# Two spectral and attention layers on one core: row blocks turned by transposing transfers instead of TensorE, and one of GpSimd's pieces moved within its batch

## The chip, the core and the metric

The kernel runs on one NeuronCore of a Trainium2 chip. Its engines work side by side and meet at semaphores: TensorE (PE; PEld is its weight load), VectorE (DVE), ScalarE (ACT), GpSimd (POOL) and SyncE (SP), whose queue issues transfers. The metric is the device time of one execution in microseconds (us). Lower is better.

## The reference

One sequence of 2048 rows with 512 columns in bf16 goes through two equal pairs of layers, each layer added to its input after a layer norm:

```python
x = x + _A_ref(_layernorm(x), A_w_r, A_w_i)               # 2-D real FFT, filter, inverse FFT
x = x + _B_ref(_layernorm(x), B_wq, B_wk, B_wv, B_wo)     # attention
# _B_ref: 32 query heads of 16 columns, one key head and one value head shared by all
scores = einsum("bhqd,bkd->bhqk", q, k) * 16 ** -0.5
p = softmax(scores); o = einsum("bhqk,bkd->bhqd", p, v); out = o @ wo
```

The two lines run twice with the same weights.

## The kernel before

Everything stays on chip between load and store. `x_sb` holds the rows as 4 (r) x 4 (t) tiles of 128x512. A "row block" is the four tiles of one t, 512 rows. The program has four stages: spectral layer, attention, spectral layer, attention. "Pair 0" is the first two, "pair 1" the last two.

**The end of a spectral layer** is `blocks` (L973 to L1059). For each row block t, TensorE does the last inverse transform (`odd`, `even`, L318 and L336), ScalarE copies one half out of PSUM (L325), VectorE joins the halves and adds the residual (`rows_out`, L353, L355). For the attention behind it, each block then needs its layer norm: statistics by VectorE (`stats`, L105 and L106, once per tile), the root by ScalarE (L109), scale and shift by VectorE (`scales`, L113, L114), and the normalised rows themselves, tile by tile, by ScalarE (L129) or VectorE (L131) as `put` is told. The rows must be turned, columns to partitions, before they can be multiplied by the weights. `transposed` (L384) does half a block: eight 128x128 transposes on TensorE into one PSUM bank (L389) and a copy of 1024 columns to `xT` by the engine it is given (L392). `keys` (L394) makes the keys of a block with four matmuls (L401), which ScalarE writes to `KT` (L403); the function that it returns has VectorE take the largest key (`kmax`, L404). `values` (L406) makes the values with 16 small matmuls (L412) and four scaled copies on ScalarE (L414). `first_queries` (L416) makes the queries of the first head group, which VectorE copies out (L421). ScalarE loads the table for the exponential at L1051. `ready` (L423) makes the factor kq from the four maxima and scales the first queries with it (L425 to L427). No score can be made before that. 

The order of TensorE, ScalarE and VectorE in a spectral layer is the order of the program's lines; an engine waits in place for what its next instruction needs. Transfers that SP issues also go out in program order. PSUM has eight banks, in `blocks` three double banks (`p2`) and two single banks (`mm`). `xT` and `Z`, the input of the transform over rows, are two views of the same 16 KB per partition, `xz`.

**The attention** (`run`, L429) has 32 head groups per pair: four query blocks of 512 queries by eight groups of four heads. A head group has 64 tiles of 128 keys x 512 queries. For 45 of them ScalarE takes the exponential from PSUM (L635), in 18 steps of three and two tiles in turn; a step is the unit of the written schedule. The other 19 are done without it: VectorE turns a score into a bit pattern (`t_new`, L669), and the tile counts as the weighted sum of four images of this pattern, shifted against each other. The pattern itself is the first. Images 1 and 2 are made by VectorE for a whole batch of tiles at once (`s_new`, L684, at the batch's steps 0 and 3). The last image is made by GpSimd, tile by tile (`pool_new`, L688); these are its *pieces*. Each piece has a dependence on the latest image by VectorE (`pace`, L550), so a piece never starts before that image has ended. The 19 tiles come in three batches of 6, 7 and 6 tiles, six steps each (`DPOS`, `BSTEPS`; the first group lacks the first batch). TensorE multiplies every tile and every image with the values (`pv_step`, L648), each a fixed number of steps after it was listed: the images of a tile are listed by `share` (L485, L492), and the result is due two steps later (`LAG`).

Pieces are dealt to the six steps by the same `share`, which rounds down: batches of seven get 1, 1, 1, 1, 1, 2. Beside pieces GpSimd normalises the output of the group before (`od_new`, L580); in odd groups VectorE then turns the outputs of two groups back (`ot_new`, L586), between images 1 and 2 of the seven-tile batch. TensorE makes the queries of the next group (L370) and, in groups 9 to 12, 17 to 20 and 25 to 28, the output projection of a finished query block (L599), whose sums VectorE adds to `x_sb` (L604).

Of the kernel before, what the change touches and what calls it, by code (L numbers as in the profile page):

```python
# [12 lines left out]
P = 128  # L13
# [13 lines left out]
BSTEPS = 6  # L27
# [330 lines left out]
class Attention:  # L358
    def __init__(self, nc, tc, tabs, norm, x_sb, xz, KT, aw, small):
        self.nc, self.tc, self.tabs, self.norm, self.x_sb, self.KT, self.aw, self.small = nc, tc, tabs, norm, x_sb, KT, aw, small  # L360
        self.xT = xz.rearrange("p (c a) (b n) -> p c (a b) n", c=NC, b=4)
        self.Z = xz.rearrange("p (i t) d -> p t i d", t=T)
        self.kmax = small.tile([P, NQB], F32, tag="kmax", bufs=1)
        self.kq = small.tile([P, 2], F32, tag="kb", bufs=1)
        self.QT = {}

    def qproj(self, g, ps, cs=range(NC)):
        qb, hg = divmod(g, HG)
        for c in cs:
            self.nc.tensor.matmul(ps, lhsT=self.aw["wq"][:, c, hg, :], rhs=self.xT[:, c, 4 * qb:4 * qb + 4, :].rearrange("d k p -> d (k p)"),  # L370
                                  start=(c == 0), stop=(c == NC - 1))

    def qcast(self, ps):
# [10 lines left out]
    def transposed(self, psum, t, xn, half, engine):  # L384

        ps = psum.tile([P, 2, NC, P], BF, tag="mm", bufs=2)
        for i in range(2):
            for c in range(NC):
                self.nc.tensor.transpose(ps[:, i, c, :], xn[:, 2 * half + i, c * P:(c + 1) * P], self.tabs["EYE"][:, 0, :])  # L389
        k = 4 * t + 2 * half  # L390
        copy = engine.copy if engine is self.nc.scalar else engine.tensor_copy
        copy(out=self.xT[:, :, k:k + 2, :].rearrange("d c i p -> d i c p"), in_=ps)  # L392

    def keys(self, psum, t):  # L394

        nc, aw = self.nc, self.aw
        k0, k1 = 4 * t, 4 * t + 4
        two = psum.tile([P, 2, 512], F32, tag="p2", bufs=3)
        ps = two[:, 0, 0:(k1 - k0) * P]
        for c in range(NC):  # L400
            nc.tensor.matmul(ps, lhsT=aw["wk"][:, c, :], rhs=self.xT[:, c, k0:k1, :].rearrange("d k p -> d (k p)"),  # L401
                             start=(c == 0), stop=(c == NC - 1))
        nc.scalar.activation(out=self.KT[:, k0 * P:k1 * P], in_=ps, func=ACT.Identity, bias=self.tabs["KAB"][:, 1:2], scale=self.tabs["KAB"][:, 0:1])  # L403
        return lambda: nc.vector.tensor_reduce(out=self.kmax[:, t:t + 1], in_=ps, axis=mybir.AxisListType.X, op=ALU.max, apply_absolute_value=True)  # L404

    def values(self, psum, t):  # L406
        nc, aw = self.nc, self.aw
        two = psum.tile([P, 2, 512], F32, tag="p2", bufs=3)
        psv = two[:, 0, 0:4 * DH].rearrange("p (i d) -> p i d", d=DH)
        for i in range(4):  # L410
            for c in range(NC):
                nc.tensor.matmul(psv[:, i, :], lhsT=self.xT[:, c, 4 * t + i, :], rhs=aw["wv"][:, c, :], start=(c == 0), stop=(c == NC - 1))  # L412
# [16 lines left out]
    def run(self, row_done, work, psums):  # L429
# [242 lines left out]
        def image_step(n):  # L672
            if n in d_phase:
                g, b, k, tiles = d_phase[n]
                src, nt = tb[(g, b)].bitcast(I16), len(tiles)
                if k == 0:
                    pool_new = work.tile([P, NBT, 512], I16, tag="SP", bufs=2)
                    sb[(g, b, 3)] = pool_new
                if k in IMG:
                    i = 1 + IMG.index(k)  # L680
                    s_new = work.tile([P, NBT, 512], I16, tag="S", bufs=3)
                    sb[(g, b, i)] = s_new
                    lo = POOL2 if i == 2 else 0
                    image[0] = nc.vector.tensor_scalar(out=s_new[:, lo:nt, :], in0=src[:, lo:nt, :], scalar1=PH_OFF[i], scalar2=None, op0=ALU.add)  # L684
                    if lo:
                        pace(nc.gpsimd.tensor_scalar(out=s_new[:, 0:lo, :], in0=src[:, 0:lo, :], scalar1=1.0, scalar2=PH_OFF[i], op0=ALU.mult, op1=ALU.add))
                for i in share(nt, k):
                    pace(nc.gpsimd.tensor_scalar(out=sb[(g, b, 3)][:, i, :], in0=src[:, i, :],  # L688
                                                 scalar1=1.0, scalar2=PH_OFF[3], op0=ALU.mult, op1=ALU.add))

# [58 lines left out]
def full_kernel(ctx, tc, A_x, A_w_r, A_w_i, B_x, B_wq, B_wk, B_wv, B_wo, out, n_pairs=2):  # L749
# [37 lines left out]
    Z = xz.rearrange("p (i t) d -> p t i d", t=T)  # L787

    def weights(tmp):
        wq_raw = tmp.tile([P, 4, D], BF, tag="x4", bufs=3)  # L790
# [182 lines left out]
    def blocks(work, sp, psum, att):  # L973
# [6 lines left out]
        def new_rows():  # L980
            X_new = work.tile([P, 4, 512], BF, tag="x4", bufs=3)
            return X_new
# [6 lines left out]
            for r in rows:  # L989
                norm.stats(x_sb[:, r, t, :], r, t)  # L990

        def rows_scaled(t):
            norm.scales(t)
            X = new_rows()
            put(t, X, (A, D, A, A))
            return X

        def turn(t, xn):
            att.transposed(psum, t, xn, 0, A)
            att.transposed(psum, t, xn, 1, A)  # L1000

        sp.odd(0)
        sums(0)
# [5 lines left out]
        sp.rows_out(1)  # L1009
        sp.odd(2)  # L1010
        sums(2)
        xn0 = rows_scaled(0)
        stats(1)
        norm.root(1)
        sp.rows_out(2)
        sp.odd(3)
        sums(3)
        xn1 = rows_scaled(1)
        stats(2)
        att.transposed(psum, 0, xn0, 0, A)  # L1020
        norm.root(2)
        att.transposed(psum, 0, xn0, 1, A)
        bound0 = att.keys(psum, 0)
        sp.rows_out(3, (0,))
        stats(3, (0, 1))
        att.transposed(psum, 1, xn1, 0, A)
        norm.root(3, slice(0, 2))
        att.transposed(psum, 1, xn1, 1, A)
        sp.rows_out(3, (1,))
        norm.scales(2)  # L1030
        xn2 = new_rows()
        put(2, xn2, (D,) * 4)
# [18 lines left out]
        nc.scalar.activation(out=dmyo, in_=norm.eps, func=ACT.Exp)  # L1051
# [118 lines left out]
```

## Time and profile before

| | |
|---|---|
| runs of this kernel | 1563.38, 1563.37, 1562.22 us; median 1563.37 |
| the profiled execution | 1565.87 us |
| its span, first to last instruction | 1564.1 us |
| first attention, first to last exponential | 119.98 to 787.4 us |
| second attention | 884.50 to 1552.4 us |
| row blocks, last normalised block to first exponential | 93 to 120 us and 858 to 884.5 us |
| granted TensorE clock, mean | 0.983 |

The profile is of one execution, taken by the hardware. A timeline line gives the start from the span's beginning, the length, the engine, the line of the kernel, the operation, what it writes and reads, how many such instructions were merged, and in brackets how long the engine had been idle and what ended that. The chain of waits is followed back from the last instruction, at each step to what released it.

### The profile page before, as it was taken

How to read it: one execution, taken by the hardware profiler on the slowest of the kernel's cores; microseconds unless marked ns; L12 is line 12 of the kernel's file. 1: busy time of each engine (PE TensorE's matmuls, PEld its weight loads, DVE VectorE, ACT ScalarE, POOL GpSimd, SP SyncE). 2: the span in 40 equal slices, each digit the busy share in tenths (PEclk: the TensorE clock that was granted, in tenths of full speed). 3: DMA queues.
4: the chain of work that ended last, by engine and by line, in shares of the span. 5: the costliest groups of instructions: out<-in, count | busy, mean ns of one | idle time of the engine just before them, and what ended most of it. 6: DMA issues, size and time to landing. Idle time of an engine off the chain costs nothing.

```text
span 1564.1 us, 33013 instructions
## 1 busy us (share of the span) xinstructions
PE 1349.6 (86%) x13145; PEld 429.5 (27%) x13252; DVE 1420.6 (91%) x2279; ACT 1442.9 (92%) x1361; POOL 797.0 (51%) x1310
## 2 busy tenths in 40 slices
PE   5888888899888988898889788888998899889987
PEld 2442222222222222222234322222222222222222
DVE  6687999999999999999987889999999999999995
ACT  6659999999999999999965799999999999999996
POOL 1003555565656655665600055556556656666564
PEclk9997999999999999999999899999999999999998
DMA  8000000000000000000010000000000000000000
GB/s 278 16 1 1 2 2 1 1 1 2 1 2 1 1 1 2 1 2 1 1 41 1 1 1 2 2 1 5 5 2 5 5 4 5 5 5 5 5 5 18
DMA packets 13198, 17.21 MB, mean 11 GB/s; under 512 B 5748, under 2 KB 10484, under 8 KB 12788
## 3 DMA queue, kind: packets, MB, share of 16 engines
q1 hardware_dynamic: 12660, 14.05, 2.7%
q8 instruction: 103, 1.69, 0.4%
q0 software_dynamic: 384, 1.05, 0.2%
q14 instruction: 51, 0.42, 0.1%
HBM read 13.00 MB, written 2.10 MB: 10 GB/s over the span
## 4 chain that ended last, share of the span: by engine, by line
DVE 35%; ACT 31%; issue 14%; PE 12%; POOL 4%; DVEq 0%; POOLq 0%; ACTq 0%
ACT e L635 30%; DVE t_new L669 16%; DVE s_new L684 9%; POOL pool_new L688 4%; PE pv_new L648 4%; PE sc L546 3%; DVE st L105 1%; PE new L203 1%; DVE o L565 1%; DVE qt L376 1%; DVE ot_new L586 1%; PE dv L546 1%; PE new L294 1%; PE new L242 1%; DVE dst L353 1%
## 5 line engine op out<-in xcount | busy, mean ns | idle before, releaser
L635 ACT ACTIVATE e<-sc 128x1536 bf16<-128x1536 f32 (+1 forms) x1158 | 1316.6, 1293 | 21.7 <-PE dv L546 17.4
L688 POOL TENSOR_SCALAR pool_new<-t_new 128x512 int16<-128x512 int16 x1204 | 748.5, 644 | 719.9 <-DVE s_new L684 630.4
L669 DVE TENSOR_SCALAR t_new<-dv 128x512 uint16<-128x512 f32 x1204 | 791.5, 677 | 76.3 <-PE dv L546 61.7
L648 PE MATMUL pv_new<-e,vaug 128*32 128x512 bf16 x2892 | 595.6, 389 | 0.0
L546 PE MATMUL sc<-qt,KT 32*128 32x512 bf16 x2892 | 459.2, 388 | 115.0 <-ACT e L635 108.5
L546 PE MATMUL dv<-qt,KT 32*128 32x512 bf16 x1204 | 455.3, 387 | 21.8 <-DVE t_new L669 20.2
L648 PE MATMUL pv_new<-s_new,vaug 128*32 128x512 bf16 x2408 | 422.5, 386 | 5.9 <-DVE s_new L684 5.9
L684 DVE TENSOR_SCALAR s_new<-t_new 128x3584 int16<-128x3584 int16 (+1 forms) x380 | 386.3, 1017 | 0.1
L648 PE MATMUL pv_new<-pool_new,vaug 128*32 128x512 bf16 x1204 | 299.8, 387 | 20.8 <-POOL pool_new L688 20.8
L546 PEld LDWEIGHTS <-KT 32*128 32x128 bf16 x4096 | 156.7, 91 | 561.0 <-issue 559.4
L648 PEld LDWEIGHTS <-vaug 128*32 128x32 bf16 x7708 | 154.3, 94 | 399.3 <-issue 368.3
L648 PE MATMUL pv_new<-t_new,vaug 128*32 128x512 bf16 x1204 | 232.7, 387 | 0.0
L370 PE MATMUL ps<-xz,wq_sb 128*128 128x512 bf16 x186 | 61.5, 386 | 4.1 <-DVE t_new L669 0.4
L565 DVE STREAM_TRANSPOSE o<-pv_new 128x512 f32<-128x512 f32 x64 | 45.2, 706 | 12.2 <-PE pv_new L648 12.2
L203 PE MATMUL new<-tab_F,xz 128*128 128x512 bf16 x186 | 48.2, 404 | 3.5 <-DVE xz L167 3.3
L376 DVE TENSOR_SCALAR qt<-ps,kq 128x512 bf16<-128x512 f32 x62 | 46.0, 742 | 1.2 <-PE ps L370 1.2
L105 DVE BATCH_NORM_STATS2 st<-x_sb 128x6 f32<-128x512 bf16 x64 | 42.9, 671 | 3.6 <-DMA x_sb<-in_A_x_dram 3.5
L580 POOL TENSOR_TENSOR od_new<-o,den 128x256 bf16<-128x256 f32 x62 | 38.5, 620 | 0.0
L267 DVE TENSOR_TENSOR m<-x_new,wt 128x1024 bf16<-128x1024 bf16 x32 | 20.7, 687 | 14.3 <-ACT x_new L243 14.3
L243 ACT CAST x_new<-new 128x1024 bf16<-128x1024 f32 x16 | 16.2, 1012 | 18.4 <-PE new L242 17.0
L370 PEld LDWEIGHTS <-wq_sb 128*128 128x128 bf16 x256 | 22.0, 97 | 31.5 <-issue 16.7
L336 PE MATMUL new<-G_new,t_new 128*128 128x512 bf16 x128 | 29.9, 379 | 0.5 <-DVE G_new L303 0.4
(106 smaller groups left out, 582.0 us busy)
## 6 DMA issues: line engine op xcount, KB each, us to landing
tab_F<-const_F SPq DMA_DIRECT2D x5, 640.0 KB, 11.7
x_sb<-in_A_x_dram SPq DMA_DIRECT2D x4, 512.0 KB, 4.8
t_new<-const_IE SPq DMA_DIRECT2D x2, 1024.0 KB, 7.3
rt<-in_A_w_r_dram SPq DMA_DIRECT2D x1, 1028.0 KB, 8.4
rt<-in_A_w_i_dram SPq DMA_DIRECT2D x1, 1028.0 KB, 12.7
t_new<-const_IO SPq DMA_DIRECT2D x2, 512.0 KB, 3.3
out_dram<-x_sb SPq DMA_DIRECT2D x8, 128.0 KB, 2.0
out_dram<-x_sb POOLq DMA_DIRECT2D x8, 128.0 KB, 2.3
```

The lines of the kernel that those rows point to most:

```text
L105: self.nc.vector.bn_stats(st, x_ap)
L203: self.mm(ps, lhsT=z, rhs=tab, start=start and i == 0, stop=stop and i == len(mms) - 1)
L370: self.nc.tensor.matmul(ps, lhsT=self.aw["wq"][:, c, hg, :], rhs=self.xT[:, c, 4 * qb:4 * qb + 4, :].rearrange("d k p -> d (k p)"), start= ...
L376: self.nc.vector.tensor_scalar(out=qt, in0=ps, scalar1=self.kq[:, 1:2], scalar2=None, op0=ALU.mult)
L546: nc.tensor.matmul(dst, lhsT=KT[hs, kc * P:(kc + 1) * P], rhs=QT[g][hs, :], start=True, stop=True)
L565: nc.vector.transpose(out=o.rearrange("p c j -> p (c j)"), in_=ps)
L580: return engine.tensor_tensor(out=turned_od[g // 2][:, :, half], in0=o[:, :, 0:DH], in1=den.unsqueeze(2).broadcast_to([P, 16, DH]), op=ALU ...
L635: nc.scalar.activation(out=e[:, 0:na, :], in_=sc[:, 0:na, :], func=ACT.Exp, scale=SCALE)
L648: nc.tensor.matmul(pv[g][32 * h:32 * h + 32, :], lhsT=vaug[:, max(j, 0), kc, :], rhs=rhs, start=(first_pv[(g, h)] == u), stop=(last_pv[(g, ...
L669: nc.vector.tensor_scalar(out=tb[(g, b)][:, i, :], in0=dv, scalar1=T_MUL, scalar2=T_ADD, op0=ALU.mult, op1=ALU.add)
L684: image[0] = nc.vector.tensor_scalar(out=s_new[:, lo:nt, :], in0=src[:, lo:nt, :], scalar1=PH_OFF[i], scalar2=None, op0=ALU.add)
L688: pace(nc.gpsimd.tensor_scalar(out=sb[(g, b, 3)][:, i, :], in0=src[:, i, :], scalar1=1.0, scalar2=PH_OFF[3], op0=ALU.mult, op1=ALU.add))
```

## The change

Three things change, and the layout that they need.

1. Row blocks 0, 1 and 2 are turned by two transfers each (`turned_rows`), which SP issues and which transpose on the way from the normalised rows to `xT`; block 3 stays with `transposed`. In blocks 0 and 1 all four tiles are now normalised by ScalarE, in block 2 by VectorE, ScalarE, VectorE, ScalarE. The first half of block 3 is copied by ScalarE instead of VectorE. Keys, maxima, values and first queries are put in another order around it.
2. The pieces of a batch are dealt rounding up: batches of seven get 2, 1, 1, 1, 1, 1; batches of six are as before. When TensorE uses them does not change.
3. `values` takes a single bank (`mm`) instead of a double one (`p2`).

`xT` is now laid out by block of 128 rows first, so a half block is one contiguous run of 1024 columns, and the rows that `keys` and `qproj` read are four runs of 128 instead of one of 512. `Z` is laid out so that a row block of it still shares its place with the same row block of `xT`.

```diff
-        self.xT = xz.rearrange("p (c a) (b n) -> p c (a b) n", c=NC, b=4)
-        self.Z = xz.rearrange("p (i t) d -> p t i d", t=T)
+        self.xT = xz.rearrange("p k (c n) -> p k c n", c=NC)
+        self.Z = xz.rearrange("p (t i) d -> p t i d", t=T)
...
+    def turned_rows(self, t, xn, half):
+
+        rows, k = slice(2 * half, 2 * half + 2), 4 * t + 2 * half
+        self.nc.sync.dma_start(out=self.xT[:, k:k + 2, :, :].rearrange("d i c p -> d (i c) p"), in_=xn[:, rows, :].rearrange("p i d -> p (i d)"), transpose=True)
...
     def values(self, psum, t):
-        two = psum.tile([P, 2, 512], F32, tag="p2", bufs=3)
-        psv = two[:, 0, 0:4 * DH].rearrange("p (i d) -> p i d", d=DH)
+        psv = psum.tile([P, 4, DH], F32, tag="mm", bufs=2)
...
-                for i in share(nt, k):
+                for i in range(-(-nt * k // BSTEPS), -(-nt * (k + 1) // BSTEPS)):
                     pace(nc.gpsimd.tensor_scalar(out=sb[(g, b, 3)][:, i, :], in0=src[:, i, :],
...
+        def rows_turned(t, engines):
             norm.scales(t)
             X = new_rows()
+            for half in range(2):
+                put(t, X, engines[2 * half:2 * half + 2], (2 * half, 2 * half + 1))
+                att.turned_rows(t, X, half)
...
-        xn0 = rows_scaled(0)
+        rows_turned(0, (A,) * 4)
         stats(1)
         norm.root(1)
         sp.rows_out(2)
         sp.odd(3)
         sums(3)
-        xn1 = rows_scaled(1)
+        rows_turned(1, (A,) * 4)
+        bound0 = att.keys(psum, 0)
         stats(2)
-        att.transposed(psum, 0, xn0, 0, A)
         norm.root(2)
-        att.transposed(psum, 0, xn0, 1, A)
-        bound0 = att.keys(psum, 0)
         sp.rows_out(3, (0,))
         stats(3, (0, 1))
-        att.transposed(psum, 1, xn1, 0, A)
         norm.root(3, slice(0, 2))
-        att.transposed(psum, 1, xn1, 1, A)
         sp.rows_out(3, (1,))
-        norm.scales(2)
-        xn2 = new_rows()
-        put(2, xn2, (D,) * 4)
+        rows_turned(2, (D, A, D, A))
+        att.values(psum, 0)
         norm.scales(3, slice(0, 2))
         xn = new_rows()
         put(3, xn, (D, D), (0, 1))
-        att.values(psum, 0)
         bound1 = att.keys(psum, 1)
         stats(3, (2, 3))
-        att.transposed(psum, 2, xn2, 0, A)
         norm.root(3, slice(2, 4))
-        att.transposed(psum, 2, xn2, 1, A)
+        att.transposed(psum, 3, xn, 0, A)
+        query = att.first_queries(psum)
         bound0()
-        att.transposed(psum, 3, xn, 0, D)
+        att.values(psum, 1)
         norm.scales(3, slice(2, 4))
         put(3, xn, (D, D), (2, 3))
+        att.transposed(psum, 3, xn, 1, D)
         bound1()
-        query = att.first_queries(psum)
         bound2 = att.keys(psum, 2)
-        att.transposed(psum, 3, xn, 1, D)
+        query()
         dmyo = small.tile([P, 1], F32, tag="dmyo", bufs=1)
         nc.scalar.activation(out=dmyo, in_=norm.eps, func=ACT.Exp)
-        query()
-        att.values(psum, 1)
         bound = att.keys(psum, 3)
+        att.qabs(att.QT[0])
         bound2()
-        att.qabs(att.QT[0])
         bound()
```

More of the change, by code (lines that the diff above doesn't have):

```diff
@@ L369, in qproj @@
         for c in cs:
-            self.nc.tensor.matmul(ps, lhsT=self.aw["wq"][:, c, hg, :], rhs=self.xT[:, c, 4 * qb:4 * qb + 4, :].rearrange("d k p -> d (k p)"),
+            self.nc.tensor.matmul(ps, lhsT=self.aw["wq"][:, c, hg, :], rhs=self.xT[:, 4 * qb:4 * qb + 4, c, :],
                                   start=(c == 0), stop=(c == NC - 1))
@@ L391, in transposed @@
         copy = engine.copy if engine is self.nc.scalar else engine.tensor_copy
-        copy(out=self.xT[:, :, k:k + 2, :].rearrange("d c i p -> d i c p"), in_=ps)
+        copy(out=self.xT[:, k:k + 2, :, :], in_=ps)
+    def turned_rows(self, t, xn, half):
+        rows, k = slice(2 * half, 2 * half + 2), 4 * t + 2 * half
+        self.nc.sync.dma_start(out=self.xT[:, k:k + 2, :, :].rearrange("d i c p -> d (i c) p"), in_=xn[:, rows, :].rearrange("p i d -> p (i d)"), transpose=True)
     def keys(self, psum, t):
@@ L400, in keys @@
         for c in range(NC):
-            nc.tensor.matmul(ps, lhsT=aw["wk"][:, c, :], rhs=self.xT[:, c, k0:k1, :].rearrange("d k p -> d (k p)"),
+            nc.tensor.matmul(ps, lhsT=aw["wk"][:, c, :], rhs=self.xT[:, k0:k1, c, :],
                              start=(c == 0), stop=(c == NC - 1))
@@ L407, in values @@
         nc, aw = self.nc, self.aw
-        two = psum.tile([P, 2, 512], F32, tag="p2", bufs=3)
-        psv = two[:, 0, 0:4 * DH].rearrange("p (i d) -> p i d", d=DH)
+        psv = psum.tile([P, 4, DH], F32, tag="mm", bufs=2)
         for i in range(4):
             for c in range(NC):
-                nc.tensor.matmul(psv[:, i, :], lhsT=self.xT[:, c, 4 * t + i, :], rhs=aw["wv"][:, c, :], start=(c == 0), stop=(c == NC - 1))
+                nc.tensor.matmul(psv[:, i, :], lhsT=self.xT[:, 4 * t + i, c, :], rhs=aw["wv"][:, c, :], start=(c == 0), stop=(c == NC - 1))
         for j in range(4):
@@ L786, in full_kernel @@
     out_v = out.flatten_outer_dims().rearrange("(r p t) d -> p r t d", r=R, p=P, t=T)
-    Z = xz.rearrange("p (i t) d -> p t i d", t=T)
+    Z = xz.rearrange("p (t i) d -> p t i d", t=T)
     def weights(tmp):
@@ L990, in stats @@
                 norm.stats(x_sb[:, r, t, :], r, t)
-        def rows_scaled(t):
+        def rows_turned(t, engines):
             norm.scales(t)
             X = new_rows()
[L995 to L1000, printed above, removed]
+            for half in range(2):
+                put(t, X, engines[2 * half:2 * half + 2], (2 * half, 2 * half + 1))
+                att.turned_rows(t, X, half)
         sp.odd(0)
```

## The prediction

> **What bounds the kernel now.** I read the page's sections 1, 2 and 4 first, then the waits of ScalarE and TensorE, then the chain of waits and the timelines in two places: one pair of head groups in the attention, and the end of the row blocks before it.
>
> ```profile
> PE 1349.6 (86%) x13145; PEld 429.5 (27%) x13252; DVE 1420.6 (91%) x2279; ACT 1442.9 (92%) x1361; POOL 797.0 (51%) x1310
> ...
> ACT e L635 30%; DVE t_new L669 16%; DVE s_new L684 9%; POOL pool_new L688 4%; PE pv_new L648 4%; PE sc L546 3%; DVE st L105 1%; PE new L203 1%; DVE o L565 1%; DVE qt L376 1%; DVE ot_new L586 1%; PE dv L546 1%; PE new L294 1%; PE new L242 1%; DVE dst L353 1%
> ```
>
> ScalarE is the fullest engine, and its exponentials (L635) lead the chain that ended last; but GpSimd, busy for 51% only, stands in that chain with 4%, some 60 us. An engine that is half idle is there because others wait for it. From the waits (who waited for whom: us in total, times, longest):
>
> ```profile
> PE pv_new L648 <- POOL pool_new L688: 20.8, 24, 1.3
> ...
> ACT e L635 <- PE dv L546: 17.4, 24, 1.5
> ```
>
> In the trace's single records 18 of TensorE's 24 waits are 0.98 us long, nine in each attention (181, 222, 264, 306 us and so on), all in odd head groups; 0.8 us after each, ScalarE stands idle for 0.63. One of them, first as the chain of waits (start, length, what), then the last two of those pieces in GpSimd's timeline, then ScalarE's timeline:
>
> ```profile
> 300.87 0.98 DVE s_new L684
> 301.86 0.07 issue
> 301.93 3.08 POOL pool_new L688 x4
> 305.00 0.04 issue
> 305.05 0.40 PE pv_new L648 x4
> ```
> ```profile
> 303.09 0.62 POOL L688 TENSOR_SCALAR pool_new<-t_new 128x512 int16<-128x512 int16 x1
> 303.68 1.32 POOL L688 TENSOR_SCALAR pool_new<-t_new 128x512 int16<-128x512 int16 x1
> ```
> ```profile
> 302.87 2.38 ACT L635 ACTIVATE e<-sc 128x1536 bf16<-128x1536 f32 x2
> 305.88 1.45 ACT L635 ACTIVATE e<-sc 128x1536 bf16<-128x1536 f32 x1 [0.63 <-PE dv L546]
> ```
>
> Four pieces follow VectorE's second image (L684, at 300.80) of the seven-tile batch. Three run at 0.59 us each; the fourth starts while VectorE makes the next image (303.56, 0.96 long) and takes 1.32. TensorE wanted it at 305.05 - 0.98 = 304.07. So ScalarE's steps at 302.87, 304.20, 305.88 are 1.33 and 1.68 us; in the single records a 1024-wide exponential is else followed after 0.90. A stall costs 1.677 - 0.903 = 0.774 us.
>
> The row blocks are another matter. From 97 to 115 us the chain of waits is VectorE almost alone (L105, L353, L131); then, in the timelines of ScalarE and VectorE:
>
> ```profile
> 113.94 0.78 ACT L403 ACTIVATE KT<-two,tab_KAB 128x512 bf16<-128x512 f32 x1 [1.11 <-PE two L401]
> 114.73 1.28 ACT L1051 ACT_TABLE_LOAD   x1
> ...
> 116.79 0.78 ACT L403 ACTIVATE KT<-two,tab_KAB 128x512 bf16<-128x512 f32 x1
> ```
> ```profile
> 117.60 0.69 DVE L404 TENSOR_REDUCE kmax<-two 128x1 f32<-128x512 f32 x1 [1.07 <-ACT KT L403]
> ...
> 118.83 0.35 DVE L427 TENSOR_SCALAR qt<-qt,kq 128x512 bf16<-128x512 bf16 x1
> ```
>
> Keys of block 3, their maximum, the factor kq, the first queries: the attention starts at 119.98. The second pair repeats this to 0.1 us, ending at 884.50.
>
> **Pieces 2, 1, 1, 1, 1, 1.** Same instructions, same TensorE order; one piece moves from behind image 2 to ahead of it. Behind image 2 stand three pieces: the last ends at 303.09 + 0.62 = 303.71, before 304.07 and without meeting the next image. All 18 stalls have this pattern to 0.01 us. VectorE can carry the faster pace: it is busy for 38.4 of the 41.5 us between two stalls. Sum: 18 x 0.774 = **-13.9 us**; nothing, if another wait takes the place; -9.7, if each leaves a step of the 0.23 us kind that ends the groups with an output projection (349.28). I take the full sum.
>
> The cost is ahead of image 2. In odd groups five GpSimd operations (four pieces, one normalisation) would end 4.25 us after image 1, image 2 starts at 4.34: free. In even groups image 2 starts 3.72 after image 1 and meets the fifth (3.6 to 4.2). The nearest row is at 776.62: an image that met a running piece took 1.48 instead of 1.08. So 30 images come some 0.45 late. Cover: VectorE idles 0.21 to 0.56 two instructions later (282.64), and the next image loses its own meeting with the fourth piece (1.24 down to 0.95, at 324.38); TensorE needs that image 0.2 earlier, but then waits 0.20 for ScalarE anyway (281.75). I take 0; without the cover 30 x 0.25 = +7.5.
>
> **Row blocks, by transfer.** Per pair TensorE loses 48 of 64 transposes (L389; 6.6 of 8.8 us in all). ScalarE loses five of six copies (L392, 1.00 each) and gains four normalisations (L129, 0.71 apart). VectorE, the bound, loses four normalisations (L131, 0.33 apart) and one of two copies (0.60): 1.9 us. SyncE gains six transfers of 256 KB; an issue takes it 0.3 to 0.6 us, its queue is otherwise done since 45 us, and the tables of the next pair behind them go out at 786. Walk, with L for issue to landing:
> - Block 0: ScalarE normalises 93.45 to 96.4; the halves land by 96.4 + L. TensorE is busy with sums until 101.2, so keys 0 wait only if L > 4.8. Behind them on TensorE stands everything else.
> - Block 1: ends 102.2, lands 102.2 + L; keys 1 end near 107.3 for L = 4, and ScalarE's KT follows.
> - Block 2: VectorE reaches its scales at 106.4 (before 107.09); ScalarE ends its two rows at 108.35; landing 108.35 + L.
> - Block 3: VectorE's last rows end at 111.9 (before 113.81), TensorE transposes until 112.5, so keys 2 start at the later of 112.5 and 108.35 + L. Keys 2 (1.05), KT (0.78), table load (1.28), dmyo, KT of block 3 (0.78), maximum and factor (1.5) follow in one row: the queries are ready at 118.2 instead of 119.18, 1.0 us earlier, up to L = 4.15; each us of L beyond costs one.
>
> No row shows a transposing transfer. Nearest rows: 128 KB out takes 1.7 to 3.0 us, 512 KB in (IO, x) 3.3 and 4.8; far end, the eight small wka transfers of short runs, issued in a row over 11.22 us, 1.40 each. With 16 blocks of 128x128 in a row block that would be 22 us. I take L = 4.5, by the 512 KB rows: 0.6 per pair, **-1.2 us**; from -2 (L under 4.15) to +34 (22 us: 22 - 4.15 - 1.0 = 17 later per pair).
>
> The Trainium skill has rules on both sides. "Advanced Engine Details and Errata", section "X-Bar Transpose (TRN2)", says that transposing transfers are as fast as plain ones; by it the sum stands. "VectorE: DVE Perf Modes", section "The three transpose paths", gives 1309 ns for one 128x128 block; 16 in a row would be an estimate of 21 us, and the time some 1582. No run here shows either yet.
>
> **Values in single banks, layout.** Values 0 is scaled away (0.55) by 108.9, before values 1 wants its bank near 111: 0; uncovered 0.55 per pair. The rows read by L370 become four runs of 128 instead of one: no row of the trace has such an operand; 0, at worst four matmuls per group slowed as at half clock (0.39 to 0.61), 0.9 us under the 1.7 us per group that TensorE waits for ScalarE (108.5 / 62).
>
> **Clock.** TensorE has 0.50 of its clock from 117.8 for 13.65 us and from 1544.6 for 10.2. Less transposing may bring the first forward: keys at 0.61 instead of 0.38, some +1 per pair. The last may shift either way, some 3 us. Both inside the range.
>
> **Sum.** -13.9 - 1.2 = -15.1. The profiled execution took 1565.87 (span 1564.1, 1.8 around it), 2.5 above the median of 1563.37: 1550.8 beside it, **1548.3** beside the median.
>
> **Rivals.**
> - *The transfers land late* (slower). If blocks of 128x128 are served one after another, keys 2 hold TensorE until 108.35 + L. It decides from L = 12: then each pair loses 6.9 and eats the gain. At 22 us: 1563.4 - 13.9 + 34 = 1583. For it: the wka rows; against: the plain rows. Chance 0.10. Half-way cases (L 6 to 10, 1551 to 1559): 0.07.
> - *VectorE pays in odd groups too.* The fifth operation (3.64 to 4.25) runs beside L586, the transposition of od_new (0.70), which never met GpSimd before. If that waits as an image does, image 2 is 0.5 late, and TensorE, which already waits 0.19 for it, stalls there; some 0.3 of the 0.77 is left: 1563.4 - 5.4 - 1.2 = 1556.8. Against it: L565, the other transposition, runs beside pieces without stretching them. 0.10.
> - *The change does not free the stall*, because TensorE waits for an earlier piece: 1562. 0.05; the end of the wait, 0.06 after the fourth piece, speaks against it.
>
> Forecast 0.68. About 0.2% (3.1 us) can be told from no change. Faster 0.83 (forecast, half-way cases, odd groups less a little), same 0.07, slower 0.10. Range 1545 to 1560: it takes in the clock's 3 us, the uncovered images and the half-way cases; it leaves out the late transfers and the unfreed stall.
>
> **What would show it.** TensorE's waits for pool_new fall from 24 to about 6, and ScalarE's steps of 1.68 vanish; images 2 of even groups take about 1.5; six transfers per pair land in 4 to 5 us; first exponential near 119.4. I am wrong if keys 2 wait for a transfer by more than 2 us, if another stall of 0.6 us stands in the odd groups, or if the late images of the even groups reach ScalarE.

## The result, and the profile after

The changed kernel takes **1545.61 us** (median of four runs, 1545.29 to 1547.75), beside 1562.80 (1560.60 to 1563.38, four runs) for the kernel before on the same chip: ratio 0.9895, 95% interval 0.9878 to 0.9913. 17.2 us were gained; 15.1 were forecast, as 1548.3. The result lies inside the stated range, close to its lower end.

In the kernel after, most lines behind the diff's first part stand four further down: L635 is L639, L684 is L688, L688 is L692. The matmuls and the copy of `keys` (L401, L403) are L406 and L408, the table load (L1051) is L1046. First the same lines as before, from the page of the kernel after: the engines' busy time, and the lines of the chain that ended last.

```profile
PE 1348.7 (87%) x13115; PEld 427.4 (28%) x13156; DVE 1421.1 (92%) x2269; ACT 1435.7 (93%) x1359; POOL 778.3 (50%) x1310
...
ACT e L639 36%; DVE t_new L673 15%; DVE s_new L688 8%; PE sc L550 2%; PE pv_new L652 2%; DVE st L105 1%; PE new L203 1%; DVE o L569 1%; DVE qt L376 1%; DVE ot_new L590 1%; PE new L294 1%; PE dv L550 1%; PE new L242 1%; DVE dst L353 1%; DVE x_sb L353 1%
```

GpSimd's pieces, 4% of the chain before, are no longer among its lines. The waits of the kernel after (who for whom: us in total, times, longest) say the same:

```profile
PE two L406 <- DMA xz<-X_new: 7.7, 4, 2.7
...
ACT e L639 <- PE dv L550: 4.5, 4, 1.5
...
PE pv_new L652 <- POOL pool_new L692: 1.4, 3, 0.6
```

TensorE's 24 waits for pieces (20.8 us) are 3 (1.4 us), and ScalarE's 24 (17.4) are 4. The first line shown is new: TensorE waits four times for a transposing transfer, 2.7 us ahead of keys 1 and 0.9 to 1.3 ahead of keys 2.

One odd head group of the kernel after, GpSimd's and VectorE's timelines (start, length, engine, line, operation, how many merged):

```profile
294.20 1.20 POOL L692 TENSOR_SCALAR pool_new<-t_new 128x512 int16<-128x512 int16 x2 [1.37 <-PE ps L370]
295.37 0.62 POOL L584 TENSOR_TENSOR od_new<-o,den 128x256 bf16<-128x256 f32 x1
295.95 1.24 POOL L692 TENSOR_SCALAR pool_new<-t_new 128x512 int16<-128x512 int16 x2
```
```profile
296.66 0.70 DVE L590 STREAM_TRANSPOSE ot_new<-od_new 128x512 bf16<-128x512 bf16 x1
297.28 1.05 DVE L688 TENSOR_SCALAR s_new<-t_new 128x3584 int16<-128x3584 int16 x1
```

The fifth operation ahead of image 2 ends at 295.95 + 1.24 = 297.19, 0.09 before the image (0.08 to 0.09 in all 30 odd groups that have one). It ran beside L590, and neither was stretched: 0.62 and 0.70 us as ever.

Now the end of the row blocks, as TensorE and ScalarE saw it in the kernel after:

```profile
104.09 1.02 PE L406 MATMUL two<-xz,wka 128*128 128x512 bf16 x4 [2.72 <-DMA xz<-X_new]
...
112.41 3.30 PE L406 MATMUL two<-xz,wka 128*128 128x512 bf16 x8 [1.30 <-DMA xz<-X_new]
```
```profile
114.33 0.78 ACT L408 ACTIVATE KT<-two,tab_KAB 128x512 bf16<-128x512 f32 x1 [3.72 <-PE two L406]
115.12 1.28 ACT L1046 ACT_TABLE_LOAD   x1
...
116.53 0.76 ACT L408 ACTIVATE KT<-two,tab_KAB 128x512 bf16<-128x512 f32 x1
```

Keys 2 (112.41) wait 1.30 us for block 2's last transfer, and then take long: keys 2 and 3 are merged in that line. By stages, in the two profiled executions:

| stage, us | before | after | difference |
|---|---|---|---|
| start to the first normalised row block | 93.40 | 92.20 | -1.2 |
| row blocks, pair 0: from there to the first exponential | 26.58 | 27.50 | +0.9 |
| first attention, to its last exponential | 667.39 | 659.16 | -8.2 |
| from there to the second pair's first normalised block | 70.56 | 70.62 | +0.1 |
| row blocks, pair 1 | 26.57 | 26.80 | +0.2 |
| second attention | 667.88 | 657.38 | -10.5 |
| after the last exponential | 11.72 | 9.92 | -1.8 |

The first stage's difference is no effect of the change: in the second profile of the same kernel (see below) the first normalised block starts at 93.57. TensorE's longest wait for an input load is 9.6 us in the profile after and 10.7 in the one before. The sum of the differences is -20.5, more than the 17.2 of the medians, because the profiled execution of before (1565.87) was 3.1 us above the median of 1562.80. So: **the attention gained, and the row blocks gained nothing in these two profiles.**

### The profile page after: what moved, and what is told of

Same layout as the page of the kernel before. It is cut to its first block, busy times and chain, and to the rows that moved or that the text cites. A ratio compares the mean times of both kernels' runs of the same rounds, so it can differ in the third digit from the quotient of the medians.

```text
span 1543.6 us, 32910 instructions
## 1 busy us (share of the span) xinstructions
PE 1348.7 (87%) x13115; PEld 427.4 (28%) x13156; DVE 1421.1 (92%) x2269; ACT 1435.7 (93%) x1359; POOL 778.3 (50%) x1310
## 2 busy tenths in 40 slices
DMA packets 25870, 20.35 MB, mean 13 GB/s; under 512 B 18420, under 2 KB 23156, under 8 KB 25460
## 3 DMA queue, kind: packets, MB, share of 16 engines
q0 software_dynamic: 384, 1.05, 0.2%
## 4 chain that ended last, share of the span: by engine, by line
ACT 38%; DVE 33%; issue 16%; PE 10%; DMA 1%; POOL 0%; DVEq 0%; POOLq 0%; ACTq 0%
ACT e L639 36%; DVE t_new L673 15%; DVE s_new L688 8%; PE sc L550 2%; PE pv_new L652 2%; DVE st L105 1%; PE new L203 1%; DVE o L569 1%; DVE qt L376 1%; DVE ot_new L590 1%; PE new L294 1%; PE dv L550 1%; PE new L242 1%; DVE dst L353 1%; DVE x_sb L353 1%
## 5 line engine op out<-in xcount | busy, mean ns | idle before, releaser
L639 ACT ACTIVATE e<-sc 128x1536 bf16<-128x1536 f32 (+1 forms) x1158 | 1312.8, 1306 | 6.4 <-PE dv L550 4.5
L692 POOL TENSOR_SCALAR pool_new<-t_new 128x512 int16<-128x512 int16 x1204 | 727.7, 626 | 723.0 <-DVE s_new L688 635.6
L652 PE MATMUL pv_new<-e,vaug 128*32 128x512 bf16 x2892 | 583.9, 386 | 0.0
L688 DVE TENSOR_SCALAR s_new<-t_new 128x3584 int16<-128x3584 int16 (+1 forms) x380 | 393.1, 1035 | 0.1
L370 PE MATMUL ps<-xz,wq_sb 128*128 128x512 bf16 x248 | 65.1, 385 | 0.6 <-DVE t_new L673 0.4
L243 ACT CAST x_new<-new 128x1024 bf16<-128x1024 f32 x16 | 16.2, 1012 | 18.4 <-PE new L242 17.0
```

The costliest lines, as they stand in the source:

```text
L639: nc.scalar.activation(out=e[:, 0:na, :], in_=sc[:, 0:na, :], func=ACT.Exp, scale=SCALE)
L652: nc.tensor.matmul(pv[g][32 * h:32 * h + 32, :], lhsT=vaug[:, max(j, 0), kc, :], rhs=rhs, start=(first_pv[(g, h)] == u), stop=(last_pv[(g, ...
```

## The experiments

"Pieces alone" means the new dealing without the transfers, and so on. All ratios are to the kernel before, timed beside it on the same chip; the runs stand in four series, and the kernel after itself took 1545.61 in one and 1547.01 in another, so medians of different series are compared to 1 or 2 us only.

**The two halves apart.** The kernel before with the new dealing alone:

```diff
-                for i in share(nt, k):
+                for i in range(-(-nt * k // BSTEPS), -(-nt * (k + 1) // BSTEPS)):
```

> The kernel before with the new dealing of pieces alone (2, 1, 1, 1, 1, 1). Theory: the dealing carries the whole gain and the transfers cost some 0.6 us per pair. From the two profiles, the attentions lost 8.2 + 10.5 us and the end after the last exponential 1.8, while the stretches from the first normalised block to the first exponential grew by 0.9 and 0.2. So this kernel takes 1562.8 - 18 to 19 = 1544 to 1545 us, 1 us less than the changed kernel, with no 0.98 us wait of TensorE for GpSimd and the row blocks at 26.6 us in both pairs. Rival: the transfers bring part of the gain, by starting the attention with TensorE in another state; then this kernel is slower than the changed one by 3 us or more.

Measured: 1546.62 us (1545.18 to 1546.91), ratio 0.9882 [0.9864, 0.9901], 15.8 us under the median of before, and a little above the 1544 to 1545 expected. Its row blocks took 26.37 and 27.25. And the kernel after with that line turned back to `share(nt, k)`:

> The changed kernel with the old dealing of pieces (1, 1, 1, 1, 1, 2): transfers and single banks alone. Theory: row blocks 0.2 to 0.9 us longer per pair than before, all 18 stalls of 0.98 us back, 1562.8 + 1.1 = 1563 to 1565 us. Rival (transfers bring part of the gain): 1557 to 1561. By the prediction's own walk (last transfer landing 4.5 us after its rows): 1561.6.

Measured: 1563.28 us (1561.91 to 1565.64), ratio 0.9999 [0.9987, 1.001]. The waits of the kernel with the transfers alone:

```profile
PE pv_new L652 <- POOL pool_new L692: 21.9, 25, 1.3
...
PE two L406 <- DMA xz<-X_new: 8.1, 4, 2.7
```

All stalls are back, and the waits for the transfers stay. The dealing carries the gain; the transfers are worth nothing that can be told here, though the interval, some 2 us to either side, does not rule out the forecast 1.2. The layout and the single bank of `values` were changed along with the transfers, and no run takes these three apart.

**What in the dealing counts.** The kernel before with the doubled step moved from the sixth to the fourth, so that all four pieces still stand behind image 2 (1, 1, 1, 2, 1, 1):

```diff
-                for i in share(nt, k):
+                dealt = (0, 1, 2, 3, 5, 6, 7) if nt == 7 else tuple(nt * j // BSTEPS for j in range(BSTEPS + 1))
+                for i in range(dealt[k], dealt[k + 1]):
```

> The kernel before, with batches of seven dealt 1, 1, 1, 2, 1, 1: the last piece is due in the schedule by itself, as in the change, but four pieces still stand behind image 2. Theory (the number of pieces behind image 2 sets the stall): GpSimd runs the four back to back in any case, the fourth meets the next image, the 18 waits of 0.98 us stay, 1562 to 1564 us. Rival (what matters is that the last step has one piece instead of two): the waits go as in the change and the time is 1545.

Measured: 1563.07 us (1559.78 to 1569.04), ratio 1.0001 [0.9985, 1.0016]. One line of its waits:

```profile
PE pv_new L648 <- POOL pool_new L689: 20.9, 24, 1.3
```

24 waits as before. A last step with one piece changes nothing; four pieces behind image 2 are what makes TensorE wait.

**The same with one piece more ahead of image 2** (3, 1, 1, 1, 1, 0: `dealt = (0, 3, 4, 5, 6, 7, 7)`), which brings about the loss that the rival "VectorE pays in odd groups too" had named, though in another way: a piece meets image 2 itself, not the transposition before it:

> The kernel before, with the pieces of the seven-tile batches dealt 3, 1, 1, 1, 1, 0 and nothing else changed. Three pieces move ahead of the second image's step where the change moves two. If only the number of pieces behind image 2 decides, TensorE's waits for them go as with 2, 1, 1, 1, 1, 1, and the time is about 1546.6 (ratio 0.988). If the collisions of image and piece count too: a sixth GpSimd operation of 0.61 us ends some 4.87 us after image 1, so that it also meets the second image of the odd groups (at 4.34), which free that image of any collision in the kernel after: it should take about 1.48 instead of 1.05, some 0.43 late, and by the prediction's price for that rival TensorE stalls there for about 0.3, 18 times, 5.4 us: about 1552 (ratio 0.993). In the even groups nothing more is lost, since image 2 is met already.

Measured: 1554.76 us (1552.38 to 1556.33), ratio 0.994 [0.992, 0.9961], 8 us more than 2, 1, 1, 1, 1, 1 took in another series. VectorE, then TensorE, in an odd group of this kernel, and a line of its waits:

```profile
255.29 0.70 DVE L586 STREAM_TRANSPOSE ot_new<-od_new 128x512 bf16<-128x512 bf16 x1
255.92 1.45 DVE L684 TENSOR_SCALAR s_new<-t_new 128x3584 int16<-128x3584 int16 x1
```
```profile
257.42 0.38 PE L648 MATMUL pv_new<-s_new,vaug 128*32 128x512 bf16 x1 [0.59 <-DVE s_new L684]
```
```profile
PE pv_new L648 <- DVE s_new L684: 17.8, 30, 0.6
```

The sixth GpSimd operation runs from 4.23 to 4.84 us after image 1, image 2 starts at 4.35, and takes 1.45 instead of 1.05. The transposition ahead of it takes 0.70 as before. TensorE then waits 0.59 for the image, in 30 groups, where it waited 0.20 (5.9 us in all) in the kernel before. ScalarE's steps lose 7.2 us against pieces alone and 9.2 against the kernel after: 0.24 to 0.31 a group. The price of 0.3 was about right; the count was not 18 but all 30 odd groups with such a batch.

**The end of the second attention.** The kernel before, with the new dealing in the last head group alone:

```diff
+                up = BSTEPS - 1 if g == NG - 1 else 0
-                for i in share(nt, k):
+                for i in range((nt * k + up) // BSTEPS, (nt * (k + 1) + up) // BSTEPS):
```

> The kernel before, with the new dealing in the last head group of each pair only. Theory: the 1.3 us wait of TensorE at 1545 us in the last group brings the half clock of 1544.6 to 1554.8 us; without it the end of the second attention is 2.5 us shorter and the end behind it 1.8, so 1562.8 - 4.3 = 1558.5 us, and no stretch of granted clock 0.50 between 1545 and 1555. Rival: the half clock falls by the phase of its own windows, not by this wait; then the time stays at 1562 to 1563 and the stretch stays.

Measured: 1560.92 us (1558.96 to 1564.49), ratio 0.9986 [0.9973, 0.9998]: some 1.5 us by the medians, 2.2 by the ratio, not 4. The wait fell from 1.31 to 0.29 as expected, but the half clock at the end, which I had put down to it, does not follow from it: the kernel with 1, 1, 1, 2, 1, 1 had the same wait of 1.31 (at 1544.4) and no half clock behind it, the one with the transfers alone had both. That part of the theory falls.

**The row blocks.** In the kernel after, block 2's rows and transfers one step earlier:

```diff
-        sp.rows_out(3, (1,))
         rows_turned(2, (D, A, D, A))
+        sp.rows_out(3, (1,))
```

> The kernel after, with the normalisation of block 2's rows and their two transposing transfers issued one step earlier, ahead of VectorE's last output rows of block 3 (L357, operand (1,)). Theory: the landing of block 2's last half is what keys 2 wait for (1.30 us in the profile after, at 112.41). Issued about 1.2 us earlier it lands before TensorE has turned block 3's rows, so the wait of keys 2 for a transfer falls from 1.3 to under 0.3, and the row blocks take some 1.0 us less than in the kernel after (26.8 to 27.5 there, depending on where the half clock falls): about 26 us at full clock; the time is 1543.5 to 1545.5, 1 to 2 us under the kernel after. Rival: VectorE's own order is the bound (its last rows of block 3 come later by what is moved ahead of them), and the row blocks stay at 26.8 to 27.5, time about 1545.6.

Measured: 1544.66 us (1543.00 to 1545.67), ratio 0.9874 [0.9853, 0.9895]; row blocks 26.03 and 25.26, some 1.5 less than in the kernel after. (Its time overlaps with the kernel after's; the gain stands on the stages of the profile.) TensorE's and ScalarE's timelines:

```profile
111.67 2.81 PE L406 MATMUL two<-xz,wka 128*128 128x512 bf16 x8
```
```profile
113.62 0.78 ACT L408 ACTIVATE KT<-two,tab_KAB 128x512 bf16<-128x512 f32 x1 [2.24 <-PE two L406]
114.41 1.28 ACT L1046 ACT_TABLE_LOAD   x1
...
115.82 0.76 ACT L408 ACTIVATE KT<-two,tab_KAB 128x512 bf16<-128x512 f32 x1
```

Keys 2 no longer wait in pair 0, and 0.46 us in pair 1. So the landing of block 2 was on the path, and VectorE's order was not the bound. What ends last now is ScalarE: its table load stands between two KTs.

Instead of that, block 2 turned by TensorE (`transposed` twice, copies by ScalarE, ahead of the first half of block 3), blocks 0 and 1 by transfers:

> The kernel after, with block 2 turned by TensorE (16 transposes, two copies by ScalarE) as in the kernel before, and only blocks 0 and 1 by transfers. Theory: the late landing of block 2's last half (4.85 us after its issue) is what the row blocks lose; without it keys 2 follow TensorE's own transposes: 16 more of them cost TensorE about 2.2 us at half clock or 1.1 at full clock, and ScalarE 2.0 for copies in a stretch where it waits anyway, so the row blocks end about where the kernel after's do, within 0.7 us of 27.5 and 26.8, and the time is 1544.5 to 1546.5. Rival: the first block's transfers and the half clock that they bring (TensorE idle for 2.7 us ahead of keys 1) are the loss, in which case the row blocks get longer still, 28 us or more, since the transposes are added behind the same wait: 1547 to 1549.

Measured: 1548.23 us (1547.76 to 1549.43), ratio 0.9899 [0.9879, 0.9919]; row blocks 28.47 and 27.57, a little under one us more than in the kernel after. My theory gave up to 0.7; the rival's numbers (28 or more, 1547 to 1549) are nearer, though by its ratio the kernel can't be told from the kernel after (0.9895). A part of the loss stands where neither had it. TensorE's timeline:

```profile
109.95 1.01 PE L389 MATMUL ps<-tab_EYE,X_new 128*128 128x128 bf16 x8 [1.64 <-DVE X_new L131]
```

VectorE, named as the releaser of block 3's transposes, had made their rows by 107.05. What ended at 109.9 was ScalarE's first copy of block 2 (108.90, 0.99), which frees one of the two single banks; it stood behind the root of block 3 in ScalarE's order. That reading is argued from the order of the records; no run took the banks apart, and the half clock that the rival blames is there too (from 104.82, for 10.24).

**What an issue costs.** In the kernel after, four transfers of one row for each block instead of two of two rows:

```diff
+        for i in (2 * half, 2 * half + 1):
+            self.nc.sync.dma_start(out=self.xT[:, 4 * t + i, :, :], in_=xn[:, i, :], transpose=True)
```

> The kernel after, with each transposing transfer of two rows (256 KB, eight blocks of 128x128) split into two of one row (128 KB, four blocks): twelve a pair instead of six, same bytes. If SyncE pays for an issue by the number of blocks, each issue takes about 0.63 us instead of 1.23 to 1.34, and the last row of block 2 lands about as late as before (4.4 to 4.9 us after the first of its two issues). If it pays per instruction, each still takes about 1.25, four of a row block hold SyncE for 5 us instead of 2.5, the last row of block 2 lands some 2.5 us later, and keys 2 wait for it for about 3.8 us instead of 1.3: row blocks of 29 to 30 us. Either way the packets stay at about 12,700 more than before.

And one transfer of 512 KB for a whole block:

> The kernel after, with one transposing transfer of 512 KB for each row block, issued once all four rows are normalised, instead of two of 256 KB. From the split into rows, an issue takes SyncE 1.2 us for 128 KB as for 256 KB, and the landing is 2.5 us after the start of the issue for 128 KB, 3.3 for 256 KB. If an issue has a price per instruction, it stays at 1.2 to 1.4 us here, and a lone 512 KB lands 3.3 + 2 x 0.85 = 5.0 us after it starts; block 2's, issued near 107.5, lands near 112.5, and keys 2 wait for it about as long as in the kernel after (1.3 us). If the chip works through 128x128 blocks one after another at 0.2 us or more each, it lands later than 112.9, and keys 2 wait for over 1.8 us.

The issue lines of the kernel after, of rows, and of whole blocks (how many, median us from issue to landing; the traces lack the landing of a third of the transfers, and of nearly half of the rows):

```profile
xz<-X_new SPq DMA_TRANSPOSE x12, 3.3
```
```profile
xz<-X_new SPq DMA_TRANSPOSE x24, 2.5
```
```profile
xz<-X_new SPq DMA_TRANSPOSE x6, 4.3
```

In the single records an issue holds SyncE for 1.19 to 1.30 us at 128 KB (twice more, up to 2.1), 1.23 to 1.35 at 256 KB (twice more, up to 1.7), 1.70 to 3.25 at 512 KB. So it is a price per instruction, nearly fixed up to 256 KB. Rows: the wait of keys 2 grew to 2.2 us, not to 3.8, and that of keys 1 to 3.7; the one execution took 1549.29 us, row blocks 28.09 and 27.26. Whole blocks: block 2's landed 5.93 after the start of its issue, not 5.0, and keys 2 waited 2.06 and 1.38; its one execution took 1548.97, row blocks 27.93 and 26.39. By these single executions neither size beats 256 KB.

**A faster version.** Block 2 early as above, and the table load with its small exponential moved ahead of keys 2, where ScalarE waited 2.24 us:

```diff
+        dmyo = small.tile([P, 1], F32, tag="dmyo", bufs=1)
+        nc.scalar.activation(out=dmyo, in_=norm.eps, func=ACT.Exp)
         bound2 = att.keys(psum, 2)
         query()
-        dmyo = small.tile([P, 1], F32, tag="dmyo", bufs=1)
-        nc.scalar.activation(out=dmyo, in_=norm.eps, func=ACT.Exp)
```

> The kernel with block 2's transfers issued a step earlier (e6_early2), and with ScalarE's table load (with the small exponential that brings it, L1046) moved ahead of keys 2, into a stretch where ScalarE waits 2.24 us for keys 2. In e6_early2 ScalarE's KT of block 2 ends at 114.40, the table load takes 1.28 and its exponential 0.2, and KT of block 3 starts at 115.82, though TensorE ends keys 3 by 114.48. Theory: the transfers no longer set the end of the row blocks, ScalarE's row does: KT of block 3 starts near 114.5, and the maximum, the factor and the queries follow 1.3 earlier: row blocks of about 24.7 and 24.0 us instead of 26.03 and 25.26; 2.6 for both pairs: 1542 beside 1544.7, and 3.6 under the kernel after of the same call. Rival: something else ends just behind it (VectorE's two maxima and the query's cast, 0.7 each, in one row from 111.9 on): then 0.5 a pair is left, 1543.7.

> The kernel after once more, unchanged, beside the two kernels of this call: 1545.6, between 1545 and 1548, ratio to before 0.9895 (0.988 to 0.991). Its row blocks should take 26.8 to 27.5 us again and its attentions 657 to 660; the half clock at the end of the second attention, absent in its first profile, may or may not come back: each half-clock stretch at the end is worth some 2 us.

Measured side by side: **1541.88 us** (1541.14 to 1543.39, ratio 0.9863 [0.9841, 0.9886]) beside 1547.01 (1546.69 to 1547.66, ratio 0.9897 [0.9878, 0.9915]) for the kernel after: 5.1 us less, and the runs do not overlap. Row blocks 24.31 and 24.22, beside 27.30 and 26.05. Against block 2 early alone, timed in another series, the row blocks are 1.7 and 1.0 us shorter. ScalarE in the faster version:

```profile
110.98 1.28 ACT L1044 ACT_TABLE_LOAD   x1
...
112.65 0.78 ACT L408 ACTIVATE KT<-two,tab_KAB 128x512 bf16<-128x512 f32 x1 [0.18 <-PE two L406]
113.89 0.78 ACT L408 ACTIVATE KT<-two,tab_KAB 128x512 bf16<-128x512 f32 x1 [0.46 <-PE two L406]
```

The second KT starts 1.24 behind the first instead of 2.20. Is it the table load alone? The same move on the kernel with the new dealing and no transfers:

> The kernel before with the new dealing alone (e1_pieces) and with the table load moved ahead of keys 2, no transfers. If the early table load pays only where TensorE has keys 3 ready early, as the transfers make it, there is little here: in the kernel before keys 3 are ready near 116.7 and KT of block 3 starts at 116.79, so the row blocks stay within 0.5 us of e1_pieces (26.4 at full clock, 27.3 where the half clock is long), and the time is 1546 to 1547. If the table load was itself on the path there too, both pairs gain 1.3: 1544.

Measured: 1546.67 us (1544.76 to 1548.09), ratio 0.9893 [0.9877, 0.991]; row blocks 26.20 and 26.30, as in the kernel before (26.58 and 26.57): next to nothing. There TensorE has keys 3 ready only at 116.8, and the load was hidden. So the transfers do make room, which the order in the kernel after did not use: with it used, they are worth 4.8 us (1541.88 beside 1546.67).

## Why the prediction held, and where it did not

- **Pieces, -13.9: right, and its mechanism shown.** In ScalarE's single records all 18 steps that were 0.774 too long are gone, and the time is lost again when four pieces stay behind image 2. The term was still too small. Steps beyond ScalarE's own 1.330 and 0.903 us add up to 43.4 us before and 24.4 after, 19.0 less (16.5 to 18.0 less in the other profiles of this dealing): 13.9 for the stalls and two parts that I had not counted. One is 2.5 us at the end of the second attention, where the last batch waited 1.31 and three more steps were late (0.98 in an execution that had no half clock there). The other, some 2 us, I had seen and used only as cover: the image behind the fourth piece. VectorE and TensorE before (even group with an output projection), then VectorE after:

```profile
324.38 1.24 DVE L684 TENSOR_SCALAR s_new<-t_new 128x3072 int16<-128x3072 int16 x1
...
326.27 0.37 PE L546 MATMUL dv<-qt,KT 32*128 32x512 bf16 x1 [0.31 <-DVE t_new L669]
```
```profile
320.26 0.95 DVE L688 TENSOR_SCALAR s_new<-t_new 128x3072 int16<-128x3072 int16 x1
```

  The image no longer meets a piece, VectorE's next `t_new` comes earlier, and two steps of ScalarE lose their 0.07 and 0.10 us, in 12 groups.
- **Even groups, late images costed at 0: right.** The second image there takes what the prediction said:

```profile
317.04 1.49 DVE L688 TENSOR_SCALAR s_new<-t_new 128x3584 int16<-128x3584 int16 x1
```

  31 such images now take 1.48 or 1.49, where two did before, and ScalarE's steps show no loss above 0.05 us that recurs with them. The Trainium skill, "SBUF — State Buffer", section "SBUF: two separate sides", says that VectorE's fast modes and GpSimd exclude each other for a whole instruction. The trace agrees nearly: with three pieces dealt first, image 2 starts 0.49 before the piece beside it ends, and takes 0.40 longer.
- **Rival "VectorE pays in odd groups too": did not come.** The transposition beside the fifth operation took 0.70 as ever, and image 2 started 0.09 us behind that operation's end, the margin that the prediction had worked out (4.25 and 4.34). With one piece more the image pays.
- **Row blocks, -0.6 a pair: did not come.** The profiles show +0.9 and +0.2, a second profile of the same kernel +0.7 and -0.5, and the timed runs of the transfers alone show no gain either. The walk's order of events was right, and two of its terms failed. First **"I take L = 4.5, by the 512 KB rows"**: block 2's rows were ready at 106.85 and landed at 112.36, 5.5 us. Of these 0.66 are a wait for SyncE, which I had let issue in 0.3 to 0.6 us, and which needs 1.2 to 1.3 for each; the last transfer itself took 4.85 (4.42 in pair 1), where the first ones take 3.0 to 3.4. By the walk's "each us of L beyond costs one" that is 1.0; the rows were ready 0.3 earlier than in the walk, counted from the start of the stage, so 0.7 is left. Second, **"Keys 2 (1.05)"**, at full clock: from 112.41 to KT at 114.33 it was 1.92, 0.9 more. The two make up the 1.5 us between -0.6 and +0.9. (The first exponential, forecast near 119.4, came at 119.70, though this execution's row blocks began 1.2 earlier.) The prediction had the clock as "+1 per pair" inside its range and at nothing in its sum, and it came:

```profile
113.79 3.60 PE L406 MATMUL two<-xz,wka 128*128 128x512 bf16 x8 [1.31 <-DMA xz<-X_new]
```
```profile
870.71 1.90 PE L406 MATMUL two<-xz,wka 128*128 128x512 bf16 x8 [1.11 <-DMA xz<-X_new]
```

  These are keys 2 and 3 of the two pairs in the second profile of the kernel after: nearly the same wait, but 3.60 us at half clock and 1.90 at full clock, and row blocks of 27.30 and 26.05. In the three profiles with these transfers and this order (the two of the kernel after and the transfers alone) the four pairs with keys 2 at half clock took 0.2 to 1.0 us longer than before, and the two at full clock 0.3 and 0.5 us less, near the forecast. So the sign went with the clock. My reading is that it falls because TensorE now idles for 2.72 us ahead of keys 1. TensorE's busy time in the kernel after, then the granted clock, around that wait:

```profile
101.50:105.00 3.50, 0.91 (x4) 0.32 (x4) 3.40 (x7) 0.78 (x3) 0.00 (x0) 1.00 0.52 97
105.00:115.20 10.20, 7.09 (x44) 3.77 (x44) 7.36 (x23) 5.25 (x15) 0.00 (x0) 0.50 0.57 54
```

  (The first figures are the window, its length and TensorE's busy time; the third last is the clock.) All kernels with transfers have such a stretch in the row blocks, from 11 to 14 us after their start. Of the six without, none has one in pair 0 until 2.2 us before the first exponential, and one has it in pair 1: pieces alone, from 860.24 for 3.41 us, after TensorE had idled for 2.21 us ahead of keys 0 and been busy for 1.23 of 3.44; its row blocks took 27.25 there. In the kernel before the same idling left 1.54 of 3.42 busy (100.73 to 104.15), and the clock stayed. That idling brings it fits all of this, but it is argued, not shown by a run of its own.
- **Rival "the transfers land late": fell.** It needed L = 12; block 2 landed 5.5 us after its rows. Of the two rules of the Trainium skill, the one of "Advanced Engine Details and Errata", section "X-Bar Transpose (TRN2)", is the nearer: 3.3 us for 256 KB lies within the plain rows (1.7 to 3.0 for 128 KB, 3.3 and 4.8 for 512 KB). By the 1309 ns of the Trainium skill's "VectorE: DVE Perf Modes", section "The three transpose paths", the eight blocks would have needed an estimated 10.5.
- **Values, layout: 0, nothing seen against it.** With the transfers and the new layout, without the new dealing, the attention is as long as before (667.84 and 667.48 beside 667.39 and 667.88). The single banks were not taken apart from the rest.
- **Clock at the end.** The tail's 1.8 us belong to the half clock of the profiled execution of before: VectorE's last transposition of sums (`o`) starts 2.50 us after the last exponential, and 0.67 in the kernel after. The transfers alone have the 2.50 too, with the same half clock; the kernels with 1, 1, 1, 2, 1, 1 and with the last group alone have neither.

The errors partly cancel: 15.1 forecast, 4.5 of gain in the attention that I had left out, less 2.3 in the row blocks (+1.1 for -1.2), make 17.3; 17.2 were measured. That it closes so well is in part luck. Some 1.5 of the 4.5 (2.5 against 0.98) belong to the half clock at the end of one execution, which the medians mostly lack, and the row blocks of the kernel after differ by 0.95 in sum between its two profiles. Timed apart, the dealing alone gained 15.8 by the medians and 18.4 by the ratio, for 13.9 forecast.

## What to carry to other kernels

A helper engine that is half idle can still set the pace: count how many of its pieces stand behind the event that releases them, and move one to where its collisions are hidden; here the margin for it was 0.09 us, and one piece more gave about half of the gain back. Work taken off an engine pays only when what ends last moves with it: here the transfers paid nothing until the last of them was issued one step earlier and the table load behind it was moved into the gap. Cost a queue's issue as an instruction of its own, by size and number, before counting on several transfers in a row.

## What the runs showed of the hardware

- A transposing transfer from SBUF to SBUF holds SyncE for about 1.2 us, whether 128 or 256 KB (most plain ones: 0.3 to 0.6, eight in the first 45 us 1.1 to 7.5), and lands 2.5, 3.3 and 4.3 us after the start of its issue for 128, 256 and 512 KB. Twelve of 256 KB add 12,672 packets (13,198 before, 25,870 after), 1056 each.
- Block 2's last transfer landed 3.9 to 4.9 us after its issue in all kernels that had it at 256 KB, where those of block 0 and the first of block 1 take 3.0 to 3.4. Why stays open.
- The half-clock stretches that end inside a profile are 3.41 us long or a multiple of it, up to 27.31, and lie differently in each execution. The Trainium skill, "TensorE: Matmul & The Clock Gate", section "What's actually happening", gives windows of some 3.4 us that run freely, an idle one bringing half clock and a busy one full clock. The lengths agree (10.24 = 3 x 3.41). But here a window with TensorE busy for 0.91 of 3.50 us was enough to bring it, and it stayed for 10.2 us in which TensorE was busy for 7.09; the measurement decides. What counts as idle is not found here: in the kernel before, stretches of 3.41 us with TensorE busy for 2.30 and 2.68 were followed by half clock as well (at 117.80 and 145.10), and others with 1.54 and 1.86 were not.
